# The order of a tile pair's run in a talking-heads attention and FFN kernel: second mixing, scores, first mixing, with value matmuls two tile pairs behind

## The chip, the cores and the metric

The kernel runs on one core of a Trainium2 chip. The metric is the device time of one execution in microseconds (us). A *ratio* below is the mean time of one kernel's fast runs over the mean of the other kernel's fast runs of the same rounds, with a 95% interval; it is therefore not quite the ratio of the medians that stand beside it.

Engines: PE is TensorE (matmuls; PEld is its weight load), DVE is VectorE, ACT is ScalarE, POOL is GpSimd, SP issues DMAs. PSUM is the memory that matmuls write to; the kernel uses it as 8 banks. A semaphore is a counter by which one engine tells another that it is done.

## The reference, cut to what matters

```python
scores = scale * np.matmul(q, k.transpose(0, 1, 3, 2))        # 8 batches, 12 heads, 448 x 448, head size 64
scores = np.einsum('bhij,hg->bgij', scores, w_pre)            # first mixing of the heads
attn = softmax(scores)                                        # over j
attn = np.einsum('bhij,hg->bgij', attn, w_post)               # second mixing of the heads
x = (attn @ v) as 3584 tokens x 768
out = np.maximum(x @ w_in, 0.0) ** 2 @ w_out                  # FFN, 768 -> 2048 -> 768
```

## The kernel before

A *tile* is 10 query rows of one batch with all 12 heads; a *step* of the main loop handles a pair of tiles, and there are 180 of them (22.5 a batch). Heads must be mixed, so the scores go to DRAM (`Sd`) and are gathered back with heads on the partitions (`G`). A step does work of four ages: scores for later tiles; the first mixing of this pair (`m_ps`), its exp, reciprocal and normalized `d`; the second mixing (`at_ps`) of the pair of two steps ago (`LAG = 2`), copied by VectorE into `at`; and, as filler for PE, matmuls of the FFN of an earlier batch. Three times a batch a *part* of `at` is complete, and two value units (`ot_ps`, 24 matmuls each) multiply it by `v`.

PE and GpSimd are given their instructions in the order of the source. ScalarE's and VectorE's are put in order by the framework's scheduler, so a change of the source's order on PE changes their order too.

```python
def score_pair(n):                         # ... cut: four matmuls into two banks
    for hh, copy in enumerate((nc.scalar.copy, nc.vector.tensor_copy)):
        copy(out=Sb[0][0:QB, 2 * (p % 2) + hh, :], in_=pss[hh][0:QB, 0:S])
    # ... cut: every second time a DMA to Sd

def mix(k):                                # first mixing: 4 matmuls into 2 PSUM banks
    pss = [bank("m_ps") for _ in range(2)]
    # ... cut: matmuls of G with pre
    for y in range(2):
        e = work.tile([P, S], F32, name="e_sb", tag="E", bufs=3)
        sm = work.tile([P, 1], F32, name="sm", tag="sm", bufs=4)
        nc.scalar.activation(out=e[:, :], in_=pss[y][:, 0:S], func=ACT.Exp, scale=SCALE, accum_out=sm[:, 0:1])
        rc = work.tile([P, 1], F32, name="rc", tag="rc", bufs=4)
        nc.vector.reciprocal(out=rc[:, :], in_=sm[:, :])
        d = dts[(2 * k + y) % ND]
        nc.gpsimd.tensor_scalar(out=d[:, 0:S], in0=e[:, :], scalar1=rc[:, 0:1], scalar2=-1.0 / S,
                                op0=ALU.mult, op1=ALU.add)
        dsb[(k, y)] = d

def unmix(k):                              # second mixing: 32 small matmuls into 2 PSUM banks
    us = [bank("at_ps") for _ in range(2)]
    # ... cut: d is the stationary operand, post the moving one
    for x, (at, c) in enumerate(places):   # ... cut: access patterns
        nc.vector.tensor_copy(out=dst, in_=src)
```

The step itself (`bank` takes the next of 8 PSUM banks in rotation, shared by all):

```python
for w, f in now:                           # timed units: value units, transposes
    f()
if now2:
    mix(ds)
scores_for(ds, ...)
if old2:
    unmix(ds - LAG)
    # ... cut: when a part is complete, its two value units are put at steps ds+1 and ds+2,
    #     and the batch's FFN is added to the filler at ds+2
gathers_for(ds)
fill(share)                                # FFN matmuls, paced
```

The softmax here doesn't subtract the row's maximum and nothing guards it: scores larger than these inputs give would overflow.

## Time and profile before

Median 630.72 us (630.18 to 631.08, 4 runs).

The page's first part (busy us, share of the span, instructions) and two rows of its second part (busy tenths in 40 slices of the span), kernel before:

```profile
PE 564.4 (89%) x11154; PEld 343.8 (54%) x11154; DVE 424.8 (67%) x1109; ACT 395.0 (63%) x1196; POOL 398.0 (63%) x579
...
PE   5247888899899999998999999998999999999997
...
DVE  4156889987876668776876678765876787656101
```

PE is the engine at its limit from about 180 us to the end. Before that PE is idle for a good part, and VectorE is the busiest engine in several slices.

The list of waits of the kernel before (engine, line, what it waited for: us in total, times, longest):

```profile
DVE rc L344 <- ACT e_sb L342: 97.1, 148, 12.9
...
PE ot_ps L177 <- DVE at L373: 14.8, 20, 2.0
...
PEld L177 <- DVE at L373: 7.5, 7, 2.1
...
PE at_ps L368 <- DVE at L373: 3.4, 13, 0.3
...
DVE at L373 <- PE at_ps L368: 2.6, 4, 1.3
...
PEld L368 <- POOL d L346: 0.5, 2, 0.3
...
PE m_ps L337 <- DVE at L373: 0.4, 1, 0.4
```

PE has waits of 14.8 and 7.5 us where value matmuls and their weight loads wait for VectorE's `at` copies. The two overlap in time (at 433.09 us both wait), so 22 us is a sign and not a loss. VectorE's `at` copy itself hardly waits for PE (2.6 us), so the copies aren't late because of their input. What VectorE does wait for is ScalarE's exp, before the reciprocal: 97.1 us.

The longest of these waits, 2.0 us, is at 60 us, in batch 0. The timeline of the kernel before around the longest one in the part where PE is the limit (start us, us busy, engine, line, instruction, count, idle time before and what ended it):

```profile
430.20 1.14 PE L259 MATMUL o_ps<-w,h 128*128 128x384 bf16 x6
430.41 1.25 POOL L346 TENSOR_SCALAR d<-e_sb,rc 128x448 bf16<-128x448 f32 x2
...
431.08 0.55 ACT L342 ACTIVATE e_sb<-m_ps 128x448 f32<-128x448 f32 x1 [1.56 <-POOL d L346]
...
431.75 0.16 DVE L344 RECIPROCAL rc<-sm 128x1 f32<-128x1 f32 x1 [1.50 <-ACT e_sb L342]
431.83 1.20 DVE L373 CAST at<-at_ps 112x480 bf16<-112x480 f32 x2
...
433.09 1.02 PE L177 MATMUL ot_ps<-at,v 112*64 112x160 bf16 x24 [1.75 <-DVE at L373]
```

Read it backwards. The value matmuls at 433.09 waited 1.75 us for the `at` copies. The two copies ran from 431.83 on, right behind a reciprocal at 431.75 that had been waiting 1.50 us for an exp; the second mixing that they copy had run from 428.83 to 429.27. The exp at 431.08 had been waiting 1.56 us for one of its three buffers, which GpSimd's `d` releases (430.41). So a value unit on PE waited for GpSimd, through two engines, although the copies have nothing to do with that exp: they only stood behind its reciprocal in VectorE's queue.

Same view, at 209 to 211 us:

```profile
209.13 0.16 DVE L344 RECIPROCAL rc<-sm 128x1 f32<-128x1 f32 x1 [0.59 <-ACT e_sb L342]
209.21 1.20 DVE L373 CAST at<-at_ps 112x480 bf16<-112x480 f32 x2
...
209.78 0.38 PE L337 MATMUL m_ps<-G,pre 60*64 60x448 bf16 x4
...
210.00 0.36 PE L302 MATMUL s_ps<-kT,qT 64*64 64x448 bf16 x4
...
210.19 0.71 PE L368 MATMUL at_ps<-post,d 60*64 60x60 bf16 x32
```

The 32 `at_ps` matmuls take 0.71 us here, against 0.44 us where nothing disturbs. The start times of the single matmuls tell that the first two start at 210.19 and the third, the first one into the second bank, only at 210.47. That is 0.06 us after the previous step's `at` copies end (209.21 + 1.20 = 210.41).

The table of stretches (us busy and instructions of each engine; PEclk is the share of TensorE's full clock that was granted) for the kernel before from the first mixing of pair 50 to that of pair 170:

```profile
core 0: us, PE busy (x) PEld busy (x) DVE busy (x) ACT busy (x) POOL busy (x), PEclk, DMA share, GB/s
182.00:552.20 370.20, 356.02 (x7207) 211.71 (x7203) 268.82 (x680) 262.32 (x792) 257.79 (x367) 1.00 0.74 186
```

### The profile page before, as it was taken

What the parts mean: (1) busy time and instruction counts of PE and PEld (TensorE: products, weight loads), DVE (VectorE), ACT (ScalarE), POOL (GpSimd) and SP (SyncE); (2) the same over time, 40 slices, a digit from 0 to 9 for tenths busy, and PEclk for the clock granted to TensorE, in tenths of its full rate; (3) what the DMA queues carried; (4) which work ended last, traced back from release to release, by engine and by line L of the source; (5) the groups of instructions that cost most, each with busy time, mean ns of one, the idle gap of its engine ahead of it and who ended that gap; (6) DMA issues with size and microseconds to landing.
All of it is one profiled execution on the core that took longest, in us unless ns stands there. A gap on an engine that the chain in (4) does not pass through costs nothing.

```text
span 630.8 us, 26832 instructions
## 1 busy us (share of the span) xinstructions
PE 564.4 (89%) x11154; PEld 343.8 (54%) x11154; DVE 424.8 (67%) x1109; ACT 395.0 (63%) x1196; POOL 398.0 (63%) x579
## 2 busy tenths in 40 slices
PE   5247888899899999998999999998999999999997
PEld 3124666665555556555655456555655556556554
DVE  4156889987876668776876678765876787656101
ACT  4245667666677766786577766785577767863320
POOL 6156847657467953897367953797467855883450
PEclk9965989999999999999999999998999999999999
DMA  9999979979867996589755996589664677411102
GB/s 143 234 225 289 244 182 206 245 191 241 226 188 203 180 227 185 162 188 214 223 163 131 194 226 211 161 181 209 202 175 132 176 186 236 139 47 53 38 8 81
DMA packets 105229, 112.64 MB, mean 179 GB/s; under 512 B 9876, under 2 KB 91284, under 8 KB 105108
## 3 DMA queue, kind: packets, MB, share of 16 engines
q1 hardware_dynamic: 66162, 88.12, 46.7%
q0 software_dynamic: 38816, 22.81, 26.9%
q8 instruction: 87, 1.43, 0.9%
q14 instruction: 34, 0.28, 0.1%
q10 hardware_dynamic: 130, 0.01, 0.0%
HBM read 84.16 MB, written 49.55 MB: 212 GB/s over the span
## 4 chain that ended last, share of the span: by engine, by line
PE 56%; DVE 14%; POOL 11%; DMA 9%; ACT 6%; issue 4%; SPq 1%; DVEq 0%; ACTq 0%; POOLq 0%
PE o_ps L259 18%; PE h_ps L226 13%; DVE at L373 7%; PE ot_ps L177 7%; PE m_ps L337 6%; PE at_ps L368 5%; DMA Sd<-S 5%; POOL d L346 5%; POOL h L238 4%; ACT e_sb L342 4%; DVE S L305 3%; DMA G<-Sd 3%; PE s_ps L302 3%; PE tr_ps L154 3%; DVE rc L344 1%
## 5 line engine op out<-in xcount | busy, mean ns | idle before, releaser
L346 POOL TENSOR_SCALAR d<-e_sb,rc 128x448 bf16<-128x448 f32 x360 | 228.3, 644 | 185.2 <-DVE rc L344 182.4
L342 ACT ACTIVATE e_sb<-m_ps 128x448 f32<-128x448 f32 x360 | 194.6, 549 | 116.9 <-PE m_ps L337 94.1
L373 DVE CAST at<-at_ps 112x480 bf16<-112x480 f32 x360 | 220.6, 644 | 2.6 <-PE at_ps L368 2.6
L226 PE MATMUL h_ps<-xt,w 128*128 128x448 bf16 (+2 forms) x960 | 162.8, 317 | 2.1 <-issue 0.4
L259 PE MATMUL o_ps<-w,h 128*128 128x384 bf16 (+1 forms) x1024 | 162.7, 329 | 0.9 <-POOL h L238 0.7
L305 DVE CAST S<-s_ps 112x448 bf16<-112x448 f32 x192 | 117.0, 615 | 30.2 <-PE s_ps L302 25.4
L344 DVE RECIPROCAL rc<-sm 128x1 f32<-128x1 f32 x360 | 56.9, 159 | 104.6 <-ACT e_sb L342 97.1
L238 POOL TENSOR_TENSOR h<-hr 128x448 bf16<-128x448 f32 (+2 forms) x124 | 108.5, 883 | 23.4 <-ACT hr L236 21.9
L368 PEld LDWEIGHTS <-d 60*64 60x64 bf16 x5760 | 86.3, 111 | 46.9 <-issue 28.1
L259 PEld LDWEIGHTS <-h 128*128 128x128 bf16 (+1 forms) x1024 | 83.1, 101 | 52.1 <-issue 2.6
L226 PEld LDWEIGHTS <-w 128*128 128x128 bf16 x960 | 79.5, 98 | 55.4 <-issue 2.9
L305 ACT CAST S<-s_ps 112x448 bf16<-112x448 f32 x192 | 101.0, 545 | 4.6 <-DMA Sd<-S 4.3
L368 PE MATMUL at_ps<-post,d 60*64 60x60 bf16 x5760 | 93.5, 194 | 11.3 <-DVE at L373 3.4
L337 PE MATMUL m_ps<-G,pre 60*64 60x448 bf16 x720 | 74.5, 385 | 19.3 <-DMA G<-Sd 17.8
L236 ACT ACTIVATE hr<-h_ps 128x448 f32<-128x448 f32 (+2 forms) x136 | 68.9, 513 | 29.6 <-PE h_ps L226 17.4
L302 PE MATMUL s_ps<-kT,qT 64*64 64x448 bf16 (+1 forms) x768 | 79.6, 377 | 5.8 <-ACT S L305 3.6
L188 ACT ACTIVATE xt<-ot_ps,bvec 128x160 bf16<-128x160 f32 (+3 forms) x144 | 44.8, 385 | 53.1 <-PE ot_ps L177 53.1
L342 ACT ACTIVATION_READ_ACCUMULATOR e_sb<-m_ps 128x1 f32 x360 | 75.3, 209 | 0.0
L177 PE MATMUL ot_ps<-at,v 112*64 112x160 bf16 (+4 forms) x1152 | 47.9, 234 | 14.8 <-DVE at L373 14.8
L177 PEld LDWEIGHTS <-v 112*64 112x64 bf16 x1152 | 40.8, 111 | 27.3 <-issue 18.8
L337 PEld LDWEIGHTS <-pre 60*64 60x64 bf16 x720 | 22.4, 105 | 59.1 <-DMA G<-Sd 25.8
L266 DVE COPY osb<-o_ps 128x384 f32<-128x384 f32 x48 | 26.5, 551 | 37.1 <-PE o_ps L259 37.1
(35 smaller groups left out, 210.4 us busy)
## 6 DMA issues: line engine op xcount, KB each, us to landing
Sd<-S SPq DMA_DIRECT2D x96, 392.0 KB, 4.3
G<-Sd SPq DMA_DIRECT2D x344, 105.0 KB, 3.4
kst<-in_k_dram POOLq DMA_DIRECT2D x24, 224.0 KB, 6.6
qst<-in_q_dram POOLq DMA_DIRECT2D x24, 224.0 KB, 6.9
v<-in_v_dram POOLq DMA_DIRECT2D x24, 224.0 KB, 6.9
w<-in_moe_w_in_dram POOLq DMA_DIRECT2D x8, 384.0 KB, 13.5
w<-in_moe_w_out_dram POOLq DMA_DIRECT2D x8, 384.0 KB, 8.2
out_dram<-osb SPq DMA_DIRECT2D x8, 336.0 KB, 7.2
```

Of the source, the lines that this page charges most:

```text
L177: nc.tensor.matmul(ps[64 * hh:64 * hh + 64, TW * y + c0:TW * y + 2 + n], lhsT=vs[b][0:PR, g, r, :], rhs=at[0:PR, r, g, c0:2 + n], start=(y ...
L226: nc.tensor.matmul(ps[:, 0:n], lhsT=w1[ft // 4][:, c2, ft % 4 * 128:ft % 4 * 128 + 128], rhs=xts[b][:, c2, c0:c1], start=(c2 == 0), stop=( ...
L236: nc.scalar.activation(out=hr[:, 0:n], in_=ps[:, 0:n], func=ACT.Relu)
L238: square.tensor_tensor(out=h2ts[(b, ft)][:, c0:c1], in0=hr[:, 0:n], in1=hr[:, 0:n], op=ALU.mult)
L259: nc.tensor.matmul(dst, lhsT=h2ts[(b, ft)][:, mt * 128:mt * 128 + ROWS[mt]], rhs=w2[ft // 4][:, ft % 4, n2 * 384:(n2 + 1) * 384], start=(f ...
L302: nc.tensor.matmul(pss[hh][z:z + m, 0:S], lhsT=qTs[b][rs, p, q0:q0 + m], rhs=kTs[b][rs, p, :], start=True, stop=True)
L305: copy(out=Sb[0][0:QB, 2 * (p % 2) + hh, :], in_=pss[hh][0:QB, 0:S])
L337: nc.tensor.matmul(pss[y][64 * x:64 * x + 64, 0:S], lhsT=pre[rows, :], rhs=g[rows, x, :], start=True, stop=True)
L342: nc.scalar.activation(out=e[:, :], in_=pss[y][:, 0:S], func=ACT.Exp, scale=SCALE, accum_out=sm[:, 0:1])
L346: nc.gpsimd.tensor_scalar(out=d[:, 0:S], in0=e[:, :], scalar1=rc[:, 0:1], scalar2=-1.0 / S, op0=ALU.mult, op1=ALU.add)
L368: nc.tensor.matmul(us[x][z:z + 64, c:c + HR], lhsT=d[rows, PR * r + z:PR * r + z + 64], rhs=post[rows, :], start=True, stop=True)
L373: nc.vector.tensor_copy(out=dst, in_=src)
```

## The change

Intent: run the second mixing first in the step, ahead of the scores and the first mixing, so that its copies are done earlier; and give the value units a further step of distance from the copies. Batch 0, which has little filler, gets both its value units at the next step and its filler one step sooner.

```diff
-EARLY = [11, 19, 26]
+EARLY = [10, 18, 25]
@@
-            rest = ((NT + 1) // 2 + LAG + 1 - ds) % (NT / 2) + 1
-            if ds <= EARLY[2]:
+            rest = ((NT + 1) // 2 + LAG + 2 - ds) % (NT / 2) + 1
+            if EARLY[2] < ds <= EARLY[2] + 2:
+                rest = NT // 2
+            elif ds <= EARLY[2]:
                 rest = 1 + min(x for x in EARLY if x >= ds) - ds
@@
-            if now2:
-                mix(ds)
-            scores_for(ds, 2 if ds < NT // 2 or not now and ds % 4 == 0 else 1)
             if old2:
                 unmix(ds - LAG)
@@
-                            at_step(ds + 1 + x, u)
+                            at_step(ds + (2 + x if b1 else 1), u)
                         if b1 == 0:
-                            at_step(ds + 2, (0, lambda c=c: filler.extend(ffn1_units(0, *c))))
+                            at_step(ds + 1, (0, lambda c=c: filler.extend(ffn1_units(0, *c))))
                     if t1 == NT - 1:
                         if b1 > 0:
-                            at_step(ds + 2, (0, lambda b1=b1: filler.extend(ffn1_units(b1))))
-                        at_step(ds + 2, (0, lambda b1=b1: filler.extend(ffn2_units(b1))))
+                            at_step(ds + 3, (0, lambda b1=b1: filler.extend(ffn1_units(b1))))
+                        at_step(ds + (3 if b1 else 1), (0, lambda b1=b1: filler.extend(ffn2_units(b1))))
+            scores_for(ds, 2 if ds < NT // 2 or not now and ds % 4 == 0 else 1)
+            if now2:
+                mix(ds)
             gathers_for(ds)
```

## The prediction

> **What bounds the kernel now.** The page's first part has TensorE (PE) busy 89% of the 630.8 us span, VectorE 67%, ScalarE and GpSimd 63%. In a table of 30 us stretches PE is busy 28 to 29.8 of 30 us from 180 to 570 us; time can only come from PE's gaps there (15 us in sum). Earlier it is otherwise: 23 us of gaps lie before 60 us (12.5 us is the wait for the first gather), and from 90 to 150 us VectorE is busy 27.3 to 28.0 of 30 us. The last 37 us are the last batch's FFN alone, which the change can't touch.
>
> **What the gaps are.** In the list of waits the value matmuls (ot_ps) wait for VectorE's at copies: 14.8 us in 20 waits, and 7.5 us in 7 waits of their weight loads. By time, the first of each part's two value units is late by 0.3 to 1.8 us, the second never: about 10 us in batches 1 to 7, 3.7 us in batch 0, 1.4 us at the end. The timeline (206 to 209 us) shows why: VectorE's order is reciprocal, S copy, reciprocal, two at copies of 0.64 us; the reciprocals wait for ScalarE's exp (97.1 us in the list) and hold the copies up. (The Trainium skill, "TensorE: Matmul & The Clock Gate", section on the array's sub-arrays, says VectorE's queue is strict FIFO; this timeline agrees.) Smaller: in 28 of 130 steps the third at_ps matmul waits 0.28 us for a PSUM bank (7.8 us).
>
> **What the change does.** Nothing is added or removed; PE has 22,310 rows before and after. Built, VectorE's order becomes at, at, S, reciprocal, reciprocal: the copies start as the at_ps matmuls end. With the value units a step (3 us) later in batches 1 to 7 their wait should vanish: -10 us. Batch 0 keeps its step but gets copies earlier: -1.5 us. The 1.8 us wait at 433 us is followed by a lower clock (0.94 in 420 to 450 us): perhaps -1 us. Bank waits change places: -2 us. PE's own cost of a step stays: either order changes twice between full-array and quarter-array matmuls, about 0.1 us each.
>
> **What it costs.** The first mixing now runs late in its step and the second early, so the time from m_ps to its at_ps (median 6.4 us) loses about 1 us. GpSimd's d takes 2 to 3 us from m_ps as a rule, at most 6.9 us. Its slack before at_ps is 3.4 us at the median, 1.3 us at the 5th percentile from 180 us on, but as low as 0.05 us from 60 to 180 us. A few new waits: +1.5 us in the steady part, +2 us in batch 0. At the start scores run before the wait for the first gather (-1 us), but later ones behind the second mixing (+1 us).
>
> Sum: about -11 us on the critical path. **Predicted 619.5 us, range 611 to 627; faster by over 2% 0.40, within 2% 0.57, slower 0.03.**
>
> **What would show it.** The wait ot_ps <- at falls from 22 us to under 5 us, or stays (wrong). PE's gaps from 180 to 580 us fall from 15 to about 5 us. VectorE's wait reciprocal <- exp falls. PE's waits for GpSimd's d rise from 0.5 us to 1 to 4 us; over 8 us would mean that a lag of two pairs is too short. The last 37 us are unchanged.
>
> **What would make it wrong.** If m_ps or s_ps wait for banks in place of at_ps, or d is late in most FFN1 steps (GpSimd up to 26.4 of 30 us there), most of the gain goes. If batch 0 gains from VectorE's order too, it is more.

## The result

Median 620.78 us (619.33 to 622.11, 4 runs) against 630.72 us; ratio 0.9843, interval 0.9813 to 0.9872. It is 1.6% faster. The profile shown below is of the fastest of the four runs (619.33 us), and that of before is of one that took longer than the four (632.61 us), so the two traces differ by 13.3 us of span where the medians differ by 9.9 us.

The first line of the page's first part, changed kernel:

```profile
PE 554.3 (90%) x11154; PEld 314.6 (51%) x11154; DVE 431.8 (70%) x1109; ACT 395.3 (64%) x1196; POOL 396.7 (64%) x579
```

The list of waits, changed kernel:

```profile
DVE rc L344 <- ACT e_sb L342: 45.3, 89, 9.2
DVE at L373 <- PE at_ps L368: 44.1, 90, 1.6
...
PEld L368 <- POOL d L346: 16.7, 41, 1.7
...
PE at_ps L368 <- POOL d L346: 4.9, 13, 1.3
PE m_ps L337 <- DVE at L373: 4.9, 8, 2.0
...
PE ot_ps L177 <- DVE at L373: 1.4, 1, 1.4
...
PE at_ps L368 <- DVE at L373: 0.5, 2, 0.3
...
PEld L177 <- DVE at L373: 0.3, 1, 0.3
```

The wait of the value matmuls fell from 14.8 + 7.5 to 1.4 + 0.3 us; what is left is one wait at the very end, which both kernels have. VectorE's reciprocal waits 45.3 us in place of 97.1. VectorE's copies now wait for PE (44.1 us): they are early. `at_ps` waits for the previous copies 0.5 us in place of 3.4. New are the waits of the second mixing for GpSimd's `d`: 4.9 us of matmuls and 16.7 us of weight loads (the latter overlap other matmuls). The first mixing, now last in the step, waits for copies too: 4.9 us in place of 0.4.

The timeline of the changed kernel for the same tile pair and the same value unit:

```profile
421.28 0.52 PE L368 MATMUL at_ps<-post,d 60*64 60x60 bf16 x32
...
421.52 0.16 DVE L344 RECIPROCAL rc<-sm 128x1 f32<-128x1 f32 x1 [0.76 <-ACT e_sb L342]
...
421.63 0.36 PE L302 MATMUL s_ps<-kT,qT 64*64 64x448 bf16 x4
...
421.82 0.36 PE L337 MATMUL m_ps<-G,pre 60*64 60x448 bf16 x4
421.83 1.22 DVE L373 CAST at<-at_ps 112x480 bf16<-112x480 f32 x2 [0.15 <-PE at_ps L368]
...
423.95 0.16 DVE L344 RECIPROCAL rc<-sm 128x1 f32<-128x1 f32 x1 [0.36 <-ACT e_sb L342]
...
427.08 1.02 PE L177 MATMUL ot_ps<-at,v 112*64 112x160 bf16 x24
```

The `at` copies of the pair that completes the part (421.83) now wait for PE: they start as the second mixing ends (421.28 + 0.52 = 421.80), where before they started some 2.6 us after it. The reciprocals of the step's own exp (423.95 is the first) come behind them. The copies end at 423.05, and the value matmuls, a step further away than before, start at 427.08 without a wait. Which of the two did it, the order or the distance, this timeline can't tell; runs e1, e2 and e4 below can.

The same stretch, pair 50 to pair 170, changed kernel (columns as in that of before):

```profile
183.30:538.80 355.50, 346.36 (x7204) 187.64 (x7206) 271.51 (x682) 260.73 (x791) 256.66 (x368) 1.00 0.77 194
```

The stretch takes 355.5 us in place of 370.2, 14.7 us less, with the same matmuls. PE's idle time in it fell by only 5.0 us (370.20 - 356.02 = 14.2, then 355.50 - 346.36 = 9.1); its *busy* time fell by 9.7 us, although no matmul was removed. So PE's busy time contained waits. (Some 1.6 us of the 14.7, an estimate, are another thing: in the trace of before, TensorE had half its clock from 434.2 to 437.6 us. In e3 below, with the same order of matmuls and nearly the same waits but no half clock in this stretch, it took 368.6 us, 354.5 of them busy.) The Trainium skill, "Perfetto Trace Analysis", section "Tensor Engine Instruction (MATMUL, LD_WEIGHTS)", says that a matmul's end in the profile is an estimate and not observed; that agrees with this. For that reason the tables below go by the *start* times of consecutive matmuls, which show waits whether the profile calls the time idle or busy.

### The profile page after: what moved, and what is told of

Read it like the earlier page. It is cut to its first block, busy times and chain, and to the rows that moved or that the text cites. A ratio compares the mean times of both kernels' runs of the same rounds, so it can differ in the third digit from the quotient of the medians.

```text
span 617.5 us, 26828 instructions
## 1 busy us (share of the span) xinstructions
PE 554.3 (90%) x11154; PEld 314.6 (51%) x11154; DVE 431.8 (70%) x1109; ACT 395.3 (64%) x1196; POOL 396.7 (64%) x579
## 4 chain that ended last, share of the span: by engine, by line
PE 67%; DVE 10%; DMA 9%; POOL 8%; issue 2%; ACT 2%; SPq 0%; ACTq 0%; POOLq 0%; DVEq 0%
PE o_ps L259 22%; PE h_ps L226 19%; PE at_ps L368 8%; PE ot_ps L177 7%; DVE at L373 5%; PE m_ps L337 5%; DMA G<-Sd 4%; POOL d L346 4%; DMA Sd<-S 4%; PE s_ps L302 4%; PE tr_ps L154 3%; POOL h L238 3%; DVE S L305 2%; DMA qst<-in_q_dram 1%; DVE h L238 1%
## 5 line engine op out<-in xcount | busy, mean ns | idle before, releaser
L373 DVE CAST at<-at_ps 112x480 bf16<-112x480 f32 x360 | 219.5, 650 | 45.0 <-PE at_ps L368 44.1
L226 PE MATMUL h_ps<-xt,w 128*128 128x448 bf16 (+2 forms) x960 | 165.7, 321 | 3.1 <-DVE at L373 2.2
L305 DVE CAST S<-s_ps 112x448 bf16<-112x448 f32 x192 | 115.7, 616 | 9.5 <-DMA Sd<-S 7.7
L226 PEld LDWEIGHTS <-w 128*128 128x128 bf16 x960 | 81.3, 100 | 80.0 <-issue 31.0
L337 PE MATMUL m_ps<-G,pre 60*64 60x448 bf16 x720 | 79.9, 368 | 26.8 <-DMA G<-Sd 16.8
L368 PE MATMUL at_ps<-post,d 60*64 60x60 bf16 x5760 | 85.7, 196 | 11.9 <-ACT S L305 5.4
L368 PEld LDWEIGHTS <-d 60*64 60x64 bf16 x5760 | 64.4, 111 | 53.9 <-issue 24.7
L344 DVE RECIPROCAL rc<-sm 128x1 f32<-128x1 f32 x360 | 50.0, 156 | 47.0 <-ACT e_sb L342 45.3
L342 ACT ACTIVATION_READ_ACCUMULATOR e_sb<-m_ps 128x1 f32 x360 | 77.8, 216 | 0.0
L302 PE MATMUL s_ps<-kT,qT 64*64 64x448 bf16 (+1 forms) x768 | 72.0, 370 | 2.3 <-ACT S L305 1.3
L337 PEld LDWEIGHTS <-pre 60*64 60x64 bf16 x720 | 27.9, 108 | 43.1 <-issue 21.8
L177 PEld LDWEIGHTS <-v 112*64 112x64 bf16 x1152 | 40.3, 113 | 15.4 <-issue 14.7
```

The lines of the kernel that those rows point to most:

```text
L177: nc.tensor.matmul(ps[64 * hh:64 * hh + 64, TW * y + c0:TW * y + 2 + n], lhsT=vs[b][0:PR, g, r, :], rhs=at[0:PR, r, g, c0:2 + n], start=(y ...
L226: nc.tensor.matmul(ps[:, 0:n], lhsT=w1[ft // 4][:, c2, ft % 4 * 128:ft % 4 * 128 + 128], rhs=xts[b][:, c2, c0:c1], start=(c2 == 0), stop=( ...
L302: nc.tensor.matmul(pss[hh][z:z + m, 0:S], lhsT=qTs[b][rs, p, q0:q0 + m], rhs=kTs[b][rs, p, :], start=True, stop=True)
L337: nc.tensor.matmul(pss[y][64 * x:64 * x + 64, 0:S], lhsT=pre[rows, :], rhs=g[rows, x, :], start=True, stop=True)
L368: nc.tensor.matmul(us[x][z:z + 64, c:c + HR], lhsT=d[rows, PR * r + z:PR * r + z + 64], rhs=post[rows, :], start=True, stop=True)
```

## The experiments

Twelve runs, each timed in up to five rounds beside the kernel before. The medians of the kernel before were 629.88, 630.92 and 630.18 us in the three sessions.

| run | what it is | median us | ratio to before, interval |
|---|---|---|---|
| e1_units_only | old order, value units of batches 1 to 7 a step later | 621.71 | 0.9867, 0.9847 to 0.9887 |
| e2_order_only | new order, everything else as before | 614.63 | 0.9754, 0.9734 to 0.9774 |
| e3_banks_only | old order, banks of the second mixing asked for first | 630.25 | 1.0002, 0.9984 to 1.0020 |
| e4_vector_order | old order on PE, new order on VectorE alone | 619.98 | 0.9842, 0.9822 to 0.9863 |
| e5_order_lag3 | e2 with a lag of three pairs | 617.70 (616.28 without a slow run) | 0.9792, 0.9759 to 0.9825 |
| e6_order_batch0 | e2 with the change's part for batch 0 | 616.02 | 0.9772, 0.9748 to 0.9796 |
| e7_order_units | e2 with the later value units | 614.37 | 0.9744, 0.9719 to 0.9768 |
| e8_mix_second | second mixing, first mixing, scores | 612.46 | 0.9715, 0.9692 to 0.9738 |
| e9_change_again | the changed kernel again | 619.13 | 0.9840, 0.9813 to 0.9867 |
| e10_order_again | e2 again | 616.03 | 0.9769, 0.9748 to 0.9790 |
| e12_mix_again | e8 again | 612.19 | 0.9726, 0.9705 to 0.9748 |
| e11_relu_on_act | e8, batch 0's relus off VectorE | 612.36 | 0.9715, 0.9697 to 0.9733 |

What the traces show between pair 50 and pair 170. A value unit counts as late when its first matmul starts more than 0.02 us later than the 0.283 us that follow the matmul ahead of it where nothing waits; an `at_ps` matmul when it starts more than 0.06 us after the one before it (the spacing is about 0.01 us otherwise). The third is the first one into the second bank, the 17th the first one that needs the second `d`.

| kernel | stretch us | value units late | third at_ps late | 17th at_ps late |
|---|---|---|---|---|
| before | 370.2 | 15, 9.4 us | 28, 7.8 us | 0 |
| changed (and e9) | 355.5 (358.5) | 0 | 0 | 11, 3.3 us (11, 3.4) |
| e1_units_only | 362.0 | 0 | 37, 10.3 us | 0 |
| e2_order_only (and e10) | 355.3 (355.1) | 0 | 0 | 10, 3.5 us (10, 3.5) |
| e3_banks_only | 368.6 | 14, 9.3 us | 28, 7.8 us | 0 |
| e4_vector_order | 357.8 | 0 | 15, 5.3 us | 0 |
| e5_order_lag3 | 354.4 | 0 | 0 | 0 |
| e6_order_batch0 | 355.1 | 0 | 0 | 8, 3.4 us |
| e7_order_units | 352.9 | 0 | 0 | 10, 3.5 us |
| e8_mix_second (and e12) | 355.0 (354.2) | 0 | 0 | 5, 2.1 us (5, 2.1) |

Lateness also moves to other places. Counting every matmul that starts more than 0.06 us later than is usual between two matmuls of these kinds, in the same stretch:

| kernel | scores late | first mixing late | second mixing late, for `d` | second mixing late, else | `o_ps` late, for GpSimd's `h` |
|---|---|---|---|---|---|
| before | 5.2 us | 0.4 us | 0 | 10.3 us | 0.8 us |
| changed | 1.4 us | 5.8 us | 4.7 us | 0 | 4.2 us |
| e2_order_only | 2.7 us | 4.6 us | 6.5 us | 0 | 1.3 us |
| e5_order_lag3 | 2.5 us | 10.3 us | 0 | 0 | 2.2 us |
| e8_mix_second | 7.4 us | 0.1 us | 4.5 us | 1.2 us | 1.3 us |

### The later value units alone

```diff
-                            at_step(ds + 1 + x, u)
+                            at_step(ds + (2 if b1 else 1) + x, u)
-                            at_step(ds + 2, (0, lambda b1=b1: filler.extend(ffn1_units(b1))))
+                            at_step(ds + 3, (0, lambda b1=b1: filler.extend(ffn1_units(b1))))
-                        at_step(ds + 2, (0, lambda b1=b1: filler.extend(ffn2_units(b1))))
+                        at_step(ds + (3 if b1 else 2), (0, lambda b1=b1: filler.extend(ffn2_units(b1))))
+            # the pace (rest) follows: LAG + 2 in place of LAG + 1
```

> The kernel before with one part of the change: value units of batches 1 to 7 (and their FFN) one step later, order of a step as before. Theory A (the gain has two parts: the value units' wait, about 9.4 us between steps 50 and 170, and the bank wait of the third at_ps matmul, about 5.5 us there; the early batch loses a little): the wait ot_ps <- at goes in batches 1 to 7, the 28 late third at_ps matmuls stay; about 621.5 us (619.5 to 623.5). Rival B (the order of the step does it all, the later units do nothing): 629 to 631 us.

621.71 us, ratio 0.9867. The value units' wait is gone between pairs 50 and 170, and that stretch is 8.2 us shorter; the late third matmuls stay (37 in place of 28). Theory A as expected. The rival, that the later units do nothing, falls for the old order.

### The new order alone

```diff
-            if now2:
-                mix(ds)
-            scores_for(ds, 2 if ds < NT // 2 or not now and ds % 4 == 0 else 1)
             if old2:
                 unmix(ds - LAG)
                 # (value units as before)
+            scores_for(ds, 2 if ds < NT // 2 or not now and ds % 4 == 0 else 1)
+            if now2:
+                mix(ds)
             gathers_for(ds)
```

> The kernel before with the new order of a step alone (second mixing, scores, first mixing); value units at the steps they had. Theory A as I now refine it: with at copies first on VectorE they end 1.6 to 2.1 us after the 17th at_ps matmul, while scores, first mixing and filler give PE about 2.3 us, so the value units wait little even without being moved: about 618 to 622 us, as the whole change. Rival C (the value units must be moved for their wait to go): ot_ps <- at stays at 8 us or more, and the time is 624 to 628 us.

614.63 us, ratio 0.9754. The stretch of pair 50 to 170 is as short as with the whole change (355.3 against 355.5 us), and the total is better than the expected 618 to 622 us, and better than the whole change (the two intervals do not touch). The list of waits of this kernel:

```profile
PEld L368 <- POOL d L346: 20.5, 46, 1.7
...
PE at_ps L368 <- POOL d L346: 7.6, 18, 1.3
...
PE ot_ps L177 <- DVE at L373: 1.4, 1, 1.4
```

The value matmuls' wait is the 1.4 us at the end, with the units at the steps that they had. So the new order removes that wait by itself in the stretch; either part of the change does, and together they can remove it only once. The order also removes the late third matmuls, which the later units do not.

### VectorE's order alone

```diff
+DVE = mybir.EngineType.DVE
@@ mix: matmuls and exp stay, the reciprocal and d go into a function of their own
+    def normalize(k):
+        for y in range(2):
+            e, sm = exps.pop((k, y))
+            # ... reciprocal on VectorE, d on GpSimd
@@
-    with tc.manual_schedule(engines={PE, POOL}):
+    with tc.manual_schedule(engines={PE, POOL, DVE}):
@@ behind unmix(ds - LAG):
+            if now2:
+                normalize(ds)
             gathers_for(ds)
```

PE's and GpSimd's instructions are in the same order as in the kernel before, all of them; VectorE's order is S copy, two `at` copies, two reciprocals. ScalarE's order differs in a few places, all outside the stretch of pair 50 to 170; in that stretch the order of score copies, `at` copies and reciprocals on VectorE is the only one that differs. (`manual_schedule` keeps the engines that it names in the order of the source.)

> The kernel before with TensorE's and GpSimd's orders unchanged; VectorE alone is put in the order S, at, at, reciprocal, reciprocal. Theory (the reciprocals that wait for exp hold up the at copies, and with them the value matmuls): ot_ps <- at falls from 22 us to under 8 us, time 621 to 626 us. Rival (the copies are late for another cause, VectorE's load or the second mixing itself): ot_ps <- at stays over 14 us, time 629 us or more. Should d come too late for the second mixing, at_ps <- d rises instead.

619.98 us, ratio 0.9842, the size of the whole change's gain (0.9843) with nothing moved on PE. Two lines of its list of waits (its line numbers are one to eight higher):

```profile
DVE rc L352 <- ACT e_sb L343: 12.0, 18, 2.4
...
PE ot_ps L178 <- DVE at L381: 3.9, 4, 1.4
```

And its timeline where a part is complete:

```profile
423.20 0.62 DVE L306 CAST S<-s_ps 112x448 bf16<-112x448 f32 x1 [0.73 <-PE s_ps L303]
...
423.75 1.21 DVE L381 CAST at<-at_ps 112x480 bf16<-112x480 f32 x2
...
424.88 0.15 DVE L352 RECIPROCAL rc<-sm 128x1 f32<-128x1 f32 x1
...
425.23 0.54 ACT L343 ACTIVATE e_sb<-m_ps 128x448 f32<-128x448 f32 x1 [1.28 <-POOL d L354]
...
425.41 1.02 PE L178 MATMUL ot_ps<-at,v 112*64 112x160 bf16 x24
...
425.90 0.16 DVE L352 RECIPROCAL rc<-sm 128x1 f32<-128x1 f32 x1 [0.87 <-ACT e_sb L343]
```

The exp at 425.23 waits 1.28 us for GpSimd's `d` as it did in the kernel before, and its reciprocal at 425.90 waits 0.87 us, but the copies (423.75) have gone ahead, and the value matmuls at 425.41 follow the filler with no gap on PE. This is the direct test of the prediction's cause: the reciprocals in front of the copies made the value units late. The rival (VectorE's load, or the second mixing itself) falls. What VectorE's order alone does not do is remove the late third matmuls: 15 of 28 are left (5.3 us), and 2.5 us of stretch against the new order on PE.

### The banks of the second mixing

```diff
+            us = [bank("at_ps") for _ in range(2)] if old2 else None
             if now2:
                 mix(ds)
@@
-                unmix(ds - LAG)
+                unmix(ds - LAG, us)
```

> The kernel before, all instructions in the same order on PE, but the two PSUM banks of the second mixing are taken from the rotation at the start of the step, ahead of those of the first mixing and the scores. Theory (the 0.28 us before the third at_ps matmul is a wait for its bank, last read by ScalarE): the 28 late third matmuls go to under 8, the ot_ps <- at wait stays at some 15 to 22 us, time 624 to 628 us, or the wait appears at m_ps or s_ps instead (630). Rival (the gap belongs to the array's change from scores to quarter-array weights, not to a bank): the 28 late ones stay, 630 to 631 us.

630.25 us, ratio 1.0002, and the same 28 late third matmuls, at the same steps. At first sight the rival wins. But the trace shows that the edit did not do what it was meant to do: the third matmuls waited for the same releases in both kernels, all 28 of them ending 0.04 us after a semaphore update of VectorE or ScalarE that came with the end of a copy or an activation. Where a bank goes is evidently not settled where the source asks for it. So this run is void as a test of bank order. That the wait is for an engine's release, and not for the array's change of shape, rests on those updates, on the other 92 steps, where PE changes its shape in the same way and no third matmul is late, and on its going away with earlier copies (e4: 28 to 15, e2: 28 to 0).

### A lag of three pairs

```diff
-LAG = 2
+LAG = 3
-EARLY = [11, 19, 26]
+EARLY = [12, 20, 27]
```

> The order-only kernel (614.6 us) with the second mixing three tile pairs behind the first in place of two. Its trace has about 12 us of late second mixing matmuls released by GpSimd's d. Theory (the new order cut the time from first to second mixing so far that d comes late): those go to under 2 us and the time to 604 to 611 us. Rival (d is late because GpSimd itself is full in the FFN1 stretches; a longer lag only moves the wait to h or elsewhere): 613 to 617 us.

617.70 us over six runs, 614.74 to 624.61. The longest of them is slow; the five fast ones have a median of 616.28 us and a ratio of 0.9792. It is not shown to be faster or slower than e2, since the intervals overlap (0.9759 to 0.9825 and 0.9734 to 0.9774). The list of waits:

```profile
PEld L368 <- POOL d L346: 6.2, 18, 0.4
...
PE m_ps L337 <- ACT e_sb L342: 2.2, 3, 1.0
```

The late second mixing is gone as meant (no late 17th matmul; the matmuls' own wait for `d` is not in the list any more), and the stretch of pair 50 to 170 took 354.4 us in place of 355.3. So the wait was removed and the time did not follow: in that stretch 3.5 us of late 17th matmuls went, and late first mixings rose from 4.6 to 10.3 us, 4.5 us of it released by ScalarE's exp. In this the rival is right: the wait moved on to another place when it was taken away. (That GpSimd is full is its reason, and was not tested by itself.) The longer lag also has a price at the end, which the expectation left out: from the first mixing of pair 170 to the end it takes 79.9 us against 77.0 in e2, as the last value units and FFN come later.

### Which part of the change costs time against the order alone

```diff
@@ e6, on top of the new order: batch 0 alone
-EARLY = [11, 19, 26]
+EARLY = [10, 18, 25]
-                            at_step(ds + 1 + x, u)
+                            at_step(ds + (1 + x if b1 else 1), u)
-                            at_step(ds + 2, (0, lambda c=c: filler.extend(ffn1_units(0, *c))))
+                            at_step(ds + 1, (0, lambda c=c: filler.extend(ffn1_units(0, *c))))
@@ (ffn2 of batch 0 at ds + 1 too)
@@ e7, on top of the new order: the diff of e1
```

> The order-only kernel (614.6 us) with the change's part for batch 0 alone: both value units and the filler one step earlier, and the paces that go with it. The whole change (620.8 us) loses against order-only before step 30. Theory (the batch 0 part, not the later value units, loses the 6 us): 618.5 to 622 us, with the 30th first mixing about 130 us from the start and not 124. Rival (the later units of batches 1 to 7 lose it): 613 to 616 us.

> The order-only kernel (614.6 us) with the value units of batches 1 to 7 one step later, as in the change, batch 0 as before. Theory (with the new order the value units wait no more, so moving them does nothing): 613 to 616.5 us. Rival (the later units lose the 6 us by which the whole change is behind order-only): 618 to 622 us.

e6: 616.02 us, e7: 614.37 us. Neither loses 6 us; both theories of the e6 run missed in part (the 30th first mixing was at 127.9 us, between the two). Since the whole change had been timed in another session, it was run again beside the order alone:

> The changed kernel once more, beside order-only on the same chip, since its 620.8 us came from another job. The batch 0 part alone cost order-only 1.4 us and the later units nothing, so if parts add up the whole change is at 614.5 to 617.5 us here; if it is again at 619 us or more, the two parts lose together what neither loses alone, or the batch 0 part costs more than its own run showed.

> Order-only once more, the yardstick of this job: 613 to 616.5 us if its first run was typical. If it is at 618 us or more, the difference from the whole change was one of jobs and not of kernels.

619.13 and 616.03 us, ratios 0.9840 and 0.9769, whose intervals do not touch. So the whole change is slower than its own main part, by 0.5% (medians) to 0.7% (ratios) of the kernel's time, and neither of the two other parts alone shows it. Two pieces of it repeat in the traces. From the first mixing of pair 170 to the end, kernels with the later units and the new order take 78.7 us (changed, e9 and e7), those without 77.0 us (e2, e10 and e6): the last batches' FFN is put off by a step and 9 more of its matmuls are left for the end (e7 has made that good before pair 170, the changed kernel has not). And the changed kernel's `o_ps` matmuls start 2.4 us after the one before at 222 us and 2.1 us at 291 us, released by GpSimd's `h`, in both of its traces; e2 and e10 have one of 1.4 us, e6 and e7 none for that reason. Why the two parts do this only together was not tried and stays open.

### Another place for the scores

```diff
             if old2:
                 unmix(ds - LAG)
-            scores_for(ds, ...)
             if now2:
                 mix(ds)
+            scores_for(ds, ...)
```

> The order-only kernel (614.6 us) with the first mixing ahead of the scores: second mixing, first mixing, scores. Theory (late d is the order's main cost): d comes 0.2 us or more earlier, ScalarE runs exp ahead of the S copy, late second mixing falls from 12 us to about 8 us, time 609 to 613 us. Rival (d's lateness is set by GpSimd's own queue, or the scores then lose as much): 613 to 617 us.

> Second mixing, first mixing, scores once more, yardstick for the next run and to confirm it as the fastest: 611 to 614.5 us, 1 to 3 us under order-only. If it is level with order-only here, the place of the scores does nothing that these runs can tell.

612.46 and 612.19 us, ratios 0.9715 and 0.9726: the fastest order, 2.7 to 2.9% faster than the kernel before and, in one session, 612.19 against the whole change's 619.13 us, 1.1% faster than that. Late 17th matmuls fell from 10 to 5. (The 12 us of the expectation are all second mixings that are late for `d` in the whole run; recounted by start times they are 13.1 us in e2 and 7.8 us in e8, as expected.) The place of a wait moved once more: late first mixings went, late scores came (table above). Against the new order alone the gain is some 0.4%, at the edge of what the runs tell (the intervals of the same session, 0.9705 to 0.9748 and 0.9748 to 0.9790, meet), and the stretch of pair 50 to 170 is level (354.2 and 355.0 against 355.1 and 355.3 us); in the traces of that session most of it (3.2 of 4.1 us of span) lies before pair 51.

### VectorE's load in batch 0

```diff
-        if n < S and ft % 2:
-            nc.vector.tensor_scalar_max(out=hr[:, 0:n], in0=ps[:, 0:n], scalar1=0.0)
-        else:
-            nc.scalar.activation(out=hr[:, 0:n], in_=ps[:, 0:n], func=ACT.Relu)
+        nc.scalar.activation(out=hr[:, 0:n], in_=ps[:, 0:n], func=ACT.Relu)
```

> The same with batch 0's 24 relus taken from VectorE (7.3 us of its time) to ScalarE. Theory (VectorE's load bounds steps 12 to 50, where no order gained): steps 12 to 50 take 2 to 5 us less than the 113.9 us of the kernel it is made from, time 608 to 611.5 us. Rival (PE, banks or ScalarE bound this stretch): within 1.5 us of it, or slower, as ScalarE gets 24 times about 0.35 us more.

612.36 us beside 612.19 us. The stretches of batch 0, first e12, then e11 (the columns are those of the stretches above):

```profile
66.00:160.00 94.00, 80.98 (x2006) 53.24 (x2005) 86.33 (x241) 64.00 (x211) 65.00 (x100) 1.00 1.02 225
```

```profile
66.00:160.00 94.00, 81.78 (x2007) 53.99 (x2006) 82.64 (x217) 68.81 (x237) 63.94 (x100) 0.98 1.02 226
```

VectorE was busy 82.6 us in place of 86.3, ScalarE 68.8 in place of 64.0, and pairs 12 to 50 took 112.5 in place of 113.4 us. The 0.9 us was lost again before pair 70. VectorE's load as such was not what bounds batch 0; the rival was right.

## Why the prediction was right, and where not

The time (619.5 predicted, 620.78 measured), the range and the likeliest class, within 2%, were right. Its mechanism was right; several of its terms were not, and that the sum came within 1.3 us is partly luck, since the errors had opposite signs: the waits for banks gave more than it said, and waits for GpSimd's `d` and `h` cost more (points 3 and 6).

1. **The value units wait because reciprocals hold up VectorE's copies: right, and shown.** VectorE's order alone (e4) removed the wait in the stretch that bounds the kernel and gave 1.6%. The strict order of VectorE's queue, which the Trainium skill states ("TensorE: Matmul & The Clock Gate", section on the array's sub-arrays), is what makes it so: at 431.83 us the copies start right behind a reciprocal that had waited 1.50 us, 2.6 us after their own input was there.
2. **"With the value units a step later ... their wait should vanish: -10 us": the size was right, but the move is not needed for it.** 9.4 us went. The move does this by itself (e1), the new order does it too without moving any unit (e2), and beside the new order the move adds nothing (e7 beside e2). The prediction saw both and booked the gain on the one that could be left out.
3. **"Bank waits change places: -2 us": too small.** The 7.8 us of late third matmuls went altogether; this is the same cause again, since most of them (17 of 28) were released by the `at` copies of the step before. In the second table above, late scores, first mixings and second mixings (those for `d` left out) are 15.9 us in sum before and 7.2 us in the changed kernel. So places did change, from the second mixing and the scores to the first mixing, and 8.7 us went and not 2.
4. **"The 1.8 us wait at 433 us is followed by a lower clock ... perhaps -1 us":** the wait is gone, and the granted clock in 420 to 450 us is 1.00 in place of 0.94. But the half clock belonged to this one trace and not to the kernel: e3 has the same wait of 1.75 us (before 431.44 us) and no half clock after it. Its stretch beside that of before, 368.6 and 370.2 us, puts the worth of the half clock at about 1.6 us, an estimate.
5. **"PE's gaps from 180 to 580 us fall from 15 to about 5 us": wrong as a sign to look for.** They fell from 15.0 to 10.6 us of idle time in those 400 us. Much of the gain showed up as less *busy* time, since ends of matmuls are modelled: in the stretch of pair 50 to 170, 9.7 of 14.7 us.
6. **"PE's waits for GpSimd's d rise from 0.5 us to 1 to 4 us; over 8 us would mean that a lag of two pairs is too short": the wait was underestimated, and the conclusion drawn from it is not borne out.** The lists give 4.9 us for the matmuls and 16.7 us for weight loads. With a lag of three (e5) the matmuls' wait went, and the time did not, in part because the end grew by 2.8 us. Waits of `o_ps` for GpSimd's `h`, 4.2 us in place of 0.8, were not foreseen.
7. **That VectorE's load limits batch 0, as its busy 27.3 to 28.0 of 30 us might suggest: not supported** (e11). What bounds batch 0 stays open. That batch 0 would gain little was right: the first mixing of pair 51 started at 185.1 us before, at 186.6 and 185.8 us in the two traces of the changed kernel, and at 182.4 and 185.2 us with the new order alone. Such differences between traces of one kernel are partly the clock's: after the gaps of the start it was granted at half until 65.5 us in the trace of before, and until 71.9 and 64.3 us in the two of the changed kernel.
8. **The last 37 us:** as predicted. From the last value matmuls to the end it is 42.9 us in both kernels (630.8 - 587.9 and 617.5 - 574.6).

What the prediction did not see is that the parts of the change other than the order cost some 0.5 to 0.7% together.

## What to carry to other kernels

When the busiest engine waits for a copy, look at what stands ahead of that copy in the copying engine's queue, and at what *that* waits for: here a 0.16 us reciprocal with a 1.5 us wait cost TensorE the time, and changing the order of one other engine, with not one matmul moved, gained as much as the whole change. A wait that two edits each remove can be gained only once, so time each edit alone before keeping both. And a wait that shows on the busiest engine isn't a gain to be had until a run without it shows that the time follows.

## What the Trainium skill lacked or had wrong

- "TensorE: Matmul & The Clock Gate", the table of the clock gate's states, has the clock halved after at least one idle window of about 3.4 us. In the kernel before, a 1.75 us wait (431.3 to 433.1 us) was followed by a half clock from 434.2 to 437.6 us; in e6, waits of 0.42, 0.29 and 0.59 us between 414.5 and 417.1 us were followed by one from 417.9 to 421.3 us. The same wait of 1.75 us in e3 (before 431.44 us) and one of 1.76 us in the changed kernel (before 291.4 us) were followed by none. So waits half as long as that window, or shorter, can be followed by a half clock, and are not always; what decides it no run here shows.
- "Perfetto Trace Analysis", section "Tensor Engine Instruction (MATMUL, LD_WEIGHTS)", says that ends of matmuls are estimates, which agrees, but not how much that can hide: of 14.7 us that went between two tile pairs, 9.7 us went from PE's *busy* time with no matmul removed (about 1.5 us of it, by the trace of e3, is the half clock in the trace of before). The spacing of starts shows such waits.
- No page was found with the time that it takes to go between matmuls over the full array and over a quarter of it ("TensorEngine Tiling", section "Tiling Modes", says only that a change of tiling mode drains TensorE): a 128x128 matmul of 448 columns was followed after 0.19 us by another of its kind and after 0.28 us by a quarter-array one, so about 0.09 us for a change.
